# Float64 weights turned into float32 by three VectorE operations in place of four, with the top bits written by ScalarE as float16

## The chip, the cores and the metric

The kernel runs on one core of one Trainium2 chip. The time is that of one execution in device microseconds (us), the median over the runs. The engines are PE (TensorE matmul), PEld (its weight load), DVE (VectorE), ACT (ScalarE), POOL (GpSimd) and SP (SyncE, which issues every transfer here). Each engine takes its instructions in the order of its own list, and waits at one whose input or buffer is not ready.

## The reference

Three layers over 4 batches of 576 tokens: attention with rotated queries and keys (8 heads of 64), a gated channel layer (`k*k @ w_v` times a sigmoid gate), and a mixer (tokens, then channels) with a residual sum. The weights that matter for this change are drawn as `float32 * numpy float64 scalar`, so they arrive as float64:

```
'w_k': np.random.randn(d_model, d_ff).astype(np.float32) * (1.0 / np.sqrt(d_model))
k = np.maximum(xk @ w_k, 0.0);  v = k * k @ w_v;  r = 1 / (1 + np.exp(-(xr @ w_r)))
h = np.maximum(xt @ w_tok1, 0.0) @ w_tok2
h2 = np.maximum(u @ w_ch1, 0.0) @ w_ch2
```

All seven weight matrices have this form. [...]

## The kernel before, in words

Activations lie with the channels on the 128 partitions and 288 tokens (half a batch) along the free dimension. Every product of the two later layers is made from three matmuls on a high and a low half (`mm3`, L555: high by high, high by low, low by high), so each weight tile of 128 x 512 is also needed as a high half (`parts[:, 0]`, rounded) and a low half (`parts[:, 1]`, the rest).

The program is written stage by stage, but the order of the instructions on each engine is made by a list scheduler from readiness and priorities (`PRI`, `ahead`). A small edit can therefore move instructions that it does not touch.

Stages, in the order of time:

- Attention, 144 steps (`a_step`, L505), from 0 to about 465 us: scores on PE (L386), maximum on DVE (L392), exponential on ACT (L399), the two float16 halves of the probabilities on ACT (L75) and DVE (L418), transposes by DMA (L435), the product with the values on PE (L448). From about step 40 on, the matmuls of the gated layer's `k` and `v` (`kp`, `vp`) fill PE between the steps.
- The first weight conversion (`conv0`), beside the first steps of the attention: the 16 tiles of `w_k` and `w_v`.
- The second (`conv1`, 17 tiles: `w_r`, both token weights, the first six tiles of the channel weights), as the attention ends, with the rest of the gated layer. Then the token mixing of batch 0.
- The third (`conv2`, the 18 other channel tiles), beside the start of the last stage.
- The channel mixing (`c1p`, `co`), to the end.

A conversion (class `Conv`, L160) has four steps for each tile. Step 0 loads the raw words into the place that the finished halves will take (`words`, L182). Step 1 has ACT take the absolute value of the upper word, read as float32 (L190), into a buffer `v`. In step 2 DVE clamps it (L195), masks and shifts it (L197), puts sign and top exponent bit in (L199) and the top three bits of the lower word (L202). Step 3 has ACT round to the high half (L73 by way of `copy`) and DVE, or POOL in `conv0`, subtract to get the low half (L104). In `conv0` the buffer `v` is a PSUM bank (one, tag `acc`, shown as `cvp`), in the other two it is an SBUF tile (three, shown as `cv`); the raw words lie in SBUF throughout, so a word of every second 4 bytes is read.

Of the kernel before, what the change touches and what calls it, by code (L numbers as in the profile page):

```python
# [3 lines left out]

# [4 lines left out]
F32 = mybir.dt.float32  # L9
F32R = mybir.dt.float32r  # L10
F16 = mybir.dt.float16
I32 = mybir.dt.int32
I64 = mybir.dt.int64
ALU = mybir.AluOpType
AF = mybir.ActivationFunctionType
# [7 lines left out]
KD, KF, KC = DM // 128, DFF // 128, DCH // 128  # L23
PSCALE = 2.0 ** 14

F64_LEAST = struct.unpack("<f", struct.pack("<I", 0x38000000))[0]
F64_MOST = struct.unpack("<f", struct.pack("<I", 0x47EFFFFF))[0]

ND = 9

# [34 lines left out]
def body(tc, kin, qin, vw, tabs, ident, mu, w_k, w_v, w_r, w_t1, w_t2, w_c1, w_c2, out):  # L65
    nc = tc.nc
    PS = bass.MemoryType.PSUM
    act, dve, pool, pe, sp = nc.scalar, nc.vector, nc.gpsimd, nc.tensor, nc.sync

    def copy(e, o, i, scale=None):  # L70
        if e == "A":
            if scale is None:
                act.activation(out=o, in_=i, func=AF.Copy)  # L73
            else:
                act.activation(out=o, in_=i, func=AF.Copy, scale=scale)  # L75
        elif e == "P":
            pool.tensor_scalar(out=o, in0=i, scalar1=1.0 if scale is None else scale, scalar2=0.0,
                               op0=ALU.mult, op1=ALU.add)
        elif scale is None:
            dve.tensor_copy(o, i)  # L80
        else:
            dve.tensor_scalar(out=o, in0=i, scalar1=scale, scalar2=None, op0=ALU.mult)
# [20 lines left out]
    def tt(e, o, a, b, op):  # L103
        return (pool if e == "P" else dve).tensor_tensor(o, a, b, op=op)  # L104

    ctx = ExitStack()
    with ctx:
# [46 lines left out]
        def behind(o, name):  # L154

            if name in last:
                tc.add_manual_dep(o.ins, last[name].ins.name, mybir.DependencyInfo(
                    mybir.DependencyClass.NoSync, mybir.DependencyReason.DATA), reason="order")

        class Conv:  # L160
# [10 lines left out]
            def stage(self, j, i):  # L171
                if not 0 <= i < len(self.q):
                    return
                weights, k = self.q[i]
                src = weights.srcs[k]
                w = src.shape[1]
                wide = src.dtype == I64
                if j == 0:
                    raw = self.words[i] = weights.words(k)
                    if self.load:  # L180
                        behind(pool.memset(raw[:, 0:1], 0), self.load)
                    sp.dma_start(raw if wide else raw[:, :w], src.bitcast(I32))  # L182
                    return
                if j < 3:
                    hl = self.words[i].rearrange("p (a b) -> p a b", b=2)
                    lw, hw = hl[:, :, 0], hl[:, :, 1]
                if j == 1:
                    v = self.t[i] = (self.room or self.cv)()[:, :w]
                    if wide:
                        act.activation(out=v.bitcast(F32), in_=hw.bitcast(F32), func=AF.Abs)  # L190
                    else:
                        act.activation(out=v.bitcast(F32), in_=self.words[i][:, :w].bitcast(F32), func=AF.Copy)
                elif j == 2 and wide:
                    v = self.t[i]
                    yield lambda: dve.tensor_scalar(out=v.bitcast(F32), in0=v.bitcast(F32), scalar1=F64_LEAST,  # L195
                                                    scalar2=F64_MOST, op0=ALU.max, op1=ALU.min)
                    yield lambda: dve.tensor_scalar(out=v, in0=v, scalar1=0x07FFFFFF, scalar2=3, op0=ALU.bitwise_and,  # L197
                                                    op1=ALU.logical_shift_left)
                    yield lambda: dve.scalar_tensor_tensor(out=v, in0=hw, scalar=-0x40000000, in1=v,  # L199
                                                           op0=ALU.bitwise_and, op1=ALU.bitwise_or)  # L200
                    o = self.t[i] = self.cv()[:, :w] if self.room else v
                    yield lambda: dve.scalar_tensor_tensor(out=o, in0=lw, scalar=29, in1=v,  # L202
                                                           op0=ALU.logical_shift_right, op1=ALU.bitwise_or)
                elif j == 3:
                    dst, f = weights.take(k), self.t.pop(i).bitcast(F32)
                    copy("A", dst[:, 0], f)
                    tt(self.low, dst[:, 1], f, dst[:, 0].bitcast(F32), ALU.subtract)
# [737 lines left out]
        while not ch.done:  # L945
            b = n // (2 * KC)
# [73 lines left out]
```

## Time and profile before

| what | value |
|---|---|
| median of 3 runs | 993.18 us (988.93 to 996.47) |
| the profiled execution | 994.62 us, span 992.8 us |
| mean granted PE clock over the span | 0.953 |
| PE busy | 869.5 us (88%) |
| DVE busy | 587.5 us (59%) |
| ACT busy | 481.6 us (49%) |
| POOL busy | 421.4 us (42%) |

The span is what the trace covers; 1.8 us of the execution lie around it. A busy share is an average over stages that have different limits, so it is read stage by stage. [...]

### The profile page before, as it was taken

Reading aid. Unit: us, or ns where it says so; the run is one execution under the profiler, and the core shown is the slowest. Engines: PE = TensorE matmul, PEld = TensorE weight load, DVE = VectorE, ACT = ScalarE, POOL = GpSimd, SP = SyncE. Lnnn points to the kernel's source line nnn. Section 1 sums busy time; section 2 is a strip of 40 time slices with the busy share of each in tenths; the row PEclk is TensorE's granted clock in tenths of the full one; section 3 lists DMA queues with packets and bytes.
Section 4 is the critical chain, followed back from the end, with each engine's and each line's share of the span. In section 5 each row is a group of like instructions: output and inputs, shape, how many; then the busy total and the mean of one; then the engine's idle time right before and its main releaser. Section 6 shows DMA issues by size and latency. Waiting matters only on the chain.

```text
span 992.8 us, 17719 instructions
## 1 busy us (share of the span) xinstructions
PE 869.5 (88%) x6512; PEld 825.4 (83%) x6512; DVE 587.5 (59%) x1264; ACT 481.6 (49%) x1077; POOL 421.4 (42%) x448
## 2 busy tenths in 40 slices
PE   2645568888898988998889979999999999999997
PEld 2534456888788887997789979999999999999997
DVE  7998987777576687776995599532133211322121
ACT  3566576777576776785654555421142113211110
POOL 7456966777867587351645411410141013101010
PEclk9976577999999999999999989999999999999999
DMA  6999889999999998999910570110211001000000
GB/s 208 265 247 260 204 165 196 185 200 203 194 186 200 202 220 173 169 170 237 301 42 25 176 299 22 36 38 1 73 37 37 1 25 55 1 25 24 1 25 24
DMA packets 216182, 127.87 MB, mean 129 GB/s; under 512 B 176032, under 2 KB 194080, under 8 KB 215968
## 3 DMA queue, kind: packets, MB, share of 16 engines
q1 hardware_dynamic: 216096, 126.75, 54.2%
q8 instruction: 51, 0.84, 0.4%
q14 instruction: 35, 0.29, 0.1%
HBM read 60.90 MB, written 14.16 MB: 76 GB/s over the span
## 4 chain that ended last, share of the span: by engine, by line
PE 49%; DVE 7%; DMA 2%; issue 1%; ACT 1%; POOL 0%; SPq 0%; DVEq 0%; ACTq 0%
PE c1p L558 5%; PE c1p L559 5%; PE c1p L560 5%; PE co L558 5%; PE co L559 5%; PE co L560 5%; PE rp L558 2%; PE rp L559 2%; PE rp L560 2%; PE S L386 1%; DVE cv L199 1%; DVE cv L202 1%; DVE cv L195 1%; DVE parts L104 1%; PE vp L559 1%
## 5 line engine op out<-in xcount | busy, mean ns | idle before, releaser
L918 DVE SCALAR_TENSOR_TENSOR hs<-c1p,hs 128x288 fp32r<-128x288 f32 x96 | 43.6, 455 | 162.8 <-ACT hs L917 162.6
L399 ACT ACTIVATE S<-S,nm 128x576 f32<-128x576 f32 x144 | 102.5, 714 | 76.0 <-DVE nm L392 75.3
L917 ACT ACTIVATE hs<-c1p 128x288 fp32r<-128x288 f32 x96 | 38.9, 410 | 191.0 <-PE c1p L560 187.4
L418 DVE SCALAR_TENSOR_TENSOR p<-S,rc,p 128x576 f16<-128x576 f32 x144 | 114.5, 811 | 21.4 <-ACT p L75 20.4
L392 DVE TENSOR_REDUCE nm<-S 128x1 f32<-128x576 f32 x144 | 106.9, 750 | 29.5 <-PE S L386 29.0
L104 POOL TENSOR_TENSOR uhl<-y,uhl 128x288 fp32r<-128x288 f32 x32 | 25.5, 829 | 223.5 <-ACT uhl L73 223.5
L558 PE MATMUL c1p<-uhl,parts 128*128 128x288 f32 x384 | 115.2, 301 | 3.7 <-DVE y L104 3.7
L559 PE MATMUL c1p<-uhl,parts 128*128 128x288 f32 x384 | 114.8, 300 | 0.0
L560 PE MATMUL c1p<-uhl,parts 128*128 128x288 f32 x384 | 114.8, 299 | 0.0
L560 PE MATMUL co<-hs,parts 128*128 128x288 f32 x384 | 112.7, 296 | 0.0
L559 PE MATMUL co<-hs,parts 128*128 128x288 f32 x384 | 112.6, 296 | 0.0
L75 ACT ACTIVATE p<-S,rc 128x576 f16<-128x576 f32 x144 | 104.6, 751 | 14.7 <-issue 5.9
L558 PE MATMUL co<-hs,parts 128*128 128x288 f32 x384 | 108.1, 297 | 0.0
L386 PE MATMUL S<-kz,kq 128*128 128x288 f32 x576 | 96.7, 309 | 9.2 <-DVE p L418 5.2
L386 PE MATMUL S<-kq 64*128 64x288 f32 (+1 forms) x288 | 62.8, 389 | 43.6 <-DVE p L418 22.0
L386 PEld LDWEIGHTS S<-kz,kq 128*128 128x128 f32 x576 | 83.4, 195 | 16.4 <-issue 11.5
L386 PEld LDWEIGHTS S<-kq 64*128 64x128 f32 (+1 forms) x288 | 52.3, 257 | 52.4 <-issue 33.5
L558 PE MATMUL kp<-xs,parts 128*128 128x288 f32 x256 | 77.2, 309 | 13.2 <-ACT t L627 10.0
L448 PE MATMUL pv<-pt,vh 128*64 128x256 f16 (+1 forms) x576 | 51.0, 327 | 35.8 <-DMA pt<-p 31.8
L558 PE MATMUL vp<-k,parts 128*128 128x288 f32 x256 | 76.7, 302 | 4.4 <-ACT t L627 4.1
L559 PE MATMUL kp<-xs,parts 128*128 128x288 f32 x256 | 76.5, 300 | 3.4 <-POOL xs L104 3.2
L104 POOL TENSOR_TENSOR q<-t 128x288 f32<-128x288 f32 x64 | 48.4, 760 | 71.0 <-ACT t L627 44.6
(118 smaller groups left out, 2491.9 us busy)
## 6 DMA issues: line engine op xcount, KB each, us to landing
words<-in_w_c_dram SPq DMA_DIRECT2D x24, 512.0 KB, 6.8
rq<-in_qin_dram SPq DMA_DIRECT2D x30, 320.0 KB, 4.0
rk<-in_kin_dram SPq DMA_DIRECT2D x32, 288.0 KB, 4.1
kz<-kq SPq DMA_DIRECT2D x48, 144.0 KB, 2.9
vr<-in_vw_dram SPq DMA_DIRECT2D x16, 320.0 KB, 3.7
xd<-xT SPq DMA_DIRECT2D x16, 288.5 KB, 2.9
vd<-vt SPq DMA_DIRECT2D x32, 144.0 KB, 2.3
y<-vd SPq DMA_DIRECT2D x8, 576.0 KB, 5.3
```

The source lines that it names most:

```text
L75: act.activation(out=o, in_=i, func=AF.Copy, scale=scale)
L104: return (pool if e == "P" else dve).tensor_tensor(o, a, b, op=op)
L386: pe.matmul(p[:, h, 0:HS], lhsT=a[l, 128 * m:128 * m + 128], rhs=b[l, h * HS:(h + 1) * HS], start=(n == 0), stop=(n == 2))
L392: dve.tensor_reduce(out=nm, in_=S_t[j][:, :, 0:HS], op=ALU.max, axis=AX.XY, negate=True)
L399: act.activation(out=e, in_=e, func=AF.Exp, bias=sum_t[j], accum_out=s)
L418: dve.scalar_tensor_tensor(out=t[:, 1], in0=S_t.pop(j)[:, :, 0:HS], scalar=sum_t[j], in1=t[:, 0], op0=ALU.mult, op1=ALU.subtract)
L448: pe.matmul(p[l, 0:n], lhsT=v[:, a, l], rhs=ts[x][:, c, :], start=(i == 0), stop=(i == len(prods) - 1))
L558: pe.matmul(p, lhsT=wh, rhs=t[:, 0], start=first, stop=False)
L559: pe.matmul(p, lhsT=wh, rhs=t[:, 1], start=False, stop=False)
L560: pe.matmul(p, lhsT=wl, rhs=t[:, 0], start=False, stop=last)
L917: act.activation(out=h[:, 0], in_=p[:, 0:HS], func=AF.Relu)
L918: dve.scalar_tensor_tensor(out=h[:, 1], in0=p[:, 0:HS], scalar=0.0, in1=h[:, 0].bitcast(F32), op0=ALU.max, op1=ALU.subtract)
```

## The change: what it does

DVE masks and shifts the upper word straight from the loaded words (`hw`) into `v`; it was ACT's absolute value, clamped, that it masked before. ACT reads the same upper word as float32 and writes it back as float16, scaled by just under 1, over the top two bytes of that word, in place. The top five bits of that float16 are the sign and the top four exponent bits that the float32 needs. DVE then takes these five bits from the word (`TOP5`) and, as before, the top three bits of the lower word. The clamp is gone. The ACT instruction must come behind the first DVE one, since it overwrites what that reads, and the second DVE one behind ACT.

```
                 if j == 1:
-                    v = self.t[i] = (self.room or self.cv)()[:, :w]
+                    v = self.t[i] = (self.room if self.room and wide else self.cv)()[:, :w]
                     if wide:
-                        act.activation(out=v.bitcast(F32), in_=hw.bitcast(F32), func=AF.Abs)
+                        top = self.words[i].bitcast(F16).rearrange("p (a b) -> p a b", b=4)[:, :, 3]
+                        dve.tensor_scalar(out=v, in0=hw, scalar1=0x00FFFFFF, scalar2=3, op0=ALU.bitwise_and,
+                                          op1=ALU.logical_shift_left)
+                        act.activation(out=top, in_=hw.bitcast(F32), func=AF.Copy, scale=JUST_UNDER)
...
                 elif j == 2 and wide:
                     v = self.t[i]
-                    yield lambda: dve.tensor_scalar(out=v.bitcast(F32), in0=v.bitcast(F32), scalar1=F64_LEAST,
-                                                    scalar2=F64_MOST, op0=ALU.max, op1=ALU.min)
-                    yield lambda: dve.tensor_scalar(out=v, in0=v, scalar1=0x07FFFFFF, scalar2=3, op0=ALU.bitwise_and,
-                                                    op1=ALU.logical_shift_left)
-                    yield lambda: dve.scalar_tensor_tensor(out=v, in0=hw, scalar=-0x40000000, in1=v,
-                                                           op0=ALU.bitwise_and, op1=ALU.bitwise_or)
+                    yield lambda: dve.scalar_tensor_tensor(out=v, in0=hw, scalar=TOP5, in1=v, op0=ALU.bitwise_and,
+                                                           op1=ALU.bitwise_or)
```

In the changed kernel these are L190 (DVE mask and shift), L192 (ACT), L197 and L200 (DVE); lines behind them are two lower than before, lines ahead of them one lower.

The scheduler places the instructions anew. On DVE, the sixth tile of `w_k` in `conv0`, beside attention steps. Before:

```order
L195 TENSOR_SCALAR cvp<-cvp 128x512
L392 TENSOR_REDUCE nm<-S 128x1 x2
L406 TENSOR_SCALAR den<-S 128x1
L197 TENSOR_SCALAR cvp<-cvp 128x512
L407 RECIPROCAL rc<-den 128x1
L406 TENSOR_SCALAR den<-S 128x1
L199 SCALAR_TENSOR_TENSOR cvp<-words,cvp 128x512
L407 RECIPROCAL rc<-den 128x1
L406 TENSOR_SCALAR den<-S 128x1
L202 SCALAR_TENSOR_TENSOR cv<-words,cvp 128x512
```

The changed kernel:

```order
L190 TENSOR_SCALAR cvp<-words 128x512
L103 TENSOR_TENSOR kq<-rq,kq 128x640
L197 SCALAR_TENSOR_TENSOR cvp<-words,cvp 128x512
L200 SCALAR_TENSOR_TENSOR cv<-words,cvp 128x512
L390 TENSOR_REDUCE nm<-S 128x1
```

Between the tile's first and second DVE instruction, where ACT must do its part, stands one other instruction; over the 51 tiles it is one to six. The last tile of `conv0` is finished on DVE behind 28 of the maxima `nm`, where it was 34 before.

On DVE, the first tiles of `conv1` (`w_r`), with the last attention steps between them. Before:

```order
L195 TENSOR_SCALAR cv<-cv 128x512
L82 TENSOR_SCALAR xT<-pv,sc 128x256
L197 TENSOR_SCALAR cv<-cv 128x512
L418 SCALAR_TENSOR_TENSOR p_6512<-S,rc,p_6512 128x576
L392 TENSOR_REDUCE nm<-S 128x1
L199 SCALAR_TENSOR_TENSOR cv<-words,cv 128x512
L195 TENSOR_SCALAR cv<-cv 128x512 x2
L202 SCALAR_TENSOR_TENSOR cv<-words,cv 128x512
```

The changed kernel:

```order
L190 TENSOR_SCALAR cv<-words 128x512
L81 TENSOR_SCALAR xT<-pv,sc 128x256
L416 SCALAR_TENSOR_TENSOR p_6496<-S,rc,p_6496 128x576
L390 TENSOR_REDUCE nm<-S 128x1
L190 TENSOR_SCALAR cv<-words 128x512
L197 SCALAR_TENSOR_TENSOR cv<-words,cv 128x512
L190 TENSOR_SCALAR cv<-words 128x512
L404 TENSOR_SCALAR den<-S 128x1
L200 SCALAR_TENSOR_TENSOR cv<-words,cv 128x512
```

The two operations on `cv` alone have become one that reads `words`; the rest of the piece stands in the same order.

## Rows read from the trace of the kernel before

**Rows 1.** Page, busy time of each engine (us, share of the span, instructions).
```profile
PE 869.5 (88%) x6512; PEld 825.4 (83%) x6512; DVE 587.5 (59%) x1264; ACT 481.6 (49%) x1077; POOL 421.4 (42%) x448
```
**Rows 2.** Stretches: busy us of PE, PEld, DVE, ACT, POOL; PE clock; DMA; GB/s.
```profile
25.00:140.00 115.00, 67.26 (x384) 56.13 (x382) 103.08 (x220) 68.83 (x139) 74.60 (x65) 0.73 0.99 234
140.00:460.00 320.00, 285.53 (x2295) 262.99 (x2295) 233.99 (x540) 226.69 (x503) 206.83 (x218) 0.97 0.95 192
460.00:520.00 60.00, 48.28 (x360) 43.44 (x359) 55.41 (x104) 37.85 (x85) 31.79 (x32) 1.00 0.64 190
562.00:594.00 32.00, 26.15 (x185) 25.21 (x183) 28.68 (x58) 19.93 (x43) 9.17 (x10) 0.94 0.79 296
600.00:993.00 393.00, 387.69 (x2941) 385.93 (x2939) 118.66 (x255) 98.36 (x244) 61.15 (x72) 1.00 0.08 25
```
**Rows 3.** Groups of instructions, conv0: busy us, mean ns; idle time before them, releaser.
```profile
L195 DVE TENSOR_SCALAR cvp<-cvp 128x512 f32<-128x512 f32 x16 | 11.0, 687 | 2.2 <-ACT cvp L190 2.2
L197 DVE TENSOR_SCALAR cvp<-cvp 128x512 int32<-128x512 int32 x16 | 11.1, 692 | 0.2
L202 DVE SCALAR_TENSOR_TENSOR cv<-words,cvp 128x512 int32<-128x512 int32 x16 | 10.8, 675 | 0.0
L190 ACT ACTIVATE cvp<-words 128x512 f32<-128x512 f32 x16 | 10.1, 630 | 6.2 <-DVE cv L202 4.9 <-DMA words<-in_w_k_dram 1.3
```
**Rows 4.** Groups by shape, the 512-wide tiles of conv1 and conv2.
```profile
L195 DVE TENSOR_SCALAR cv<-cv 128x512 f32<-128x512 f32 x28 | 13.7, 491 | 5.4 <-ACT cv L190 5.4
L197 DVE TENSOR_SCALAR cv<-cv 128x512 int32<-128x512 int32 x28 | 13.9, 504 | 0.0
L199 DVE SCALAR_TENSOR_TENSOR cv<-words,cv 128x512 int32<-128x512 int32 x28 | 21.3, 768 | 0.0
L190 ACT ACTIVATE cv<-words 128x512 f32<-128x512 f32 x28 | 18.9, 679 | 14.7 <-DVE parts L104 10.0 <-DMA words<-in_w_r_dram 3.8 <-DMA words<-in_w_c_dram 0.5
```
**Rows 5.** Stretches, the instructions of L195 alone: length, DVE busy us.
```profile
25.00:140.00 115.00, 10.99 (x16) 0.73 0.99 234
460.00:520.00 60.00, 8.51 (x17) 1.00 0.64 190
562.00:594.00 32.00, 4.65 (x9) 0.94 0.79 296
```
**Rows 6.** Line L195 from 460 us on: duration min/median/max ns, first and last start.
```profile
L195 DVE TENSOR_SCALAR cv<-cv x27: 278/415/1012, 466.9 to 596.8; 128x512 f32<-128x512 f32 x20, 128x256 f32<-128x256 f32 x5, 128x576 f32<-128x576 f32 x2
```
**Rows 7.** Timeline of DVE in conv1: start us, us, operation.
```profile
507.46 0.68 DVE L202 SCALAR_TENSOR_TENSOR cv<-words,cv 128x512 int32<-128x512 int32 x1
508.06 0.41 DVE L195 TENSOR_SCALAR cv<-cv 128x512 f32<-128x512 f32 x1
508.39 0.75 DVE L197 TENSOR_SCALAR cv<-cv 128x512 int32<-128x512 int32 x2
```
**Rows 8.** Waits from 25 to 140 us: total us, times, longest.
```profile
ACT S L399 <- DVE nm L392: 26.7, 19, 4.3
PE S L386 <- DVE p L418: 17.0, 10, 6.4
```
**Rows 9.** Waits from 460 to 600 us.
```profile
ACT cv L190 <- DVE parts L104: 13.0, 11, 2.8
ACT parts L73 <- DVE cv L202: 11.7, 14, 1.5
PE kp L558 <- ACT t L627: 8.0, 7, 2.1
DVE cv L195 <- ACT cv L190: 4.5, 2, 3.3
```
**Rows 10.** Chain that ended last, as batch 0's mixing is released: start us, us, what.
```profile
592.54 0.93 DVE cv L195
593.47 0.38 DVE y L104
593.98 0.58 PE c1p L558
```

More of the change, by code (lines that the diff above doesn't have):

```diff
@@ L1 @@
-import struct
 from contextlib import ExitStack
@@ L24 @@
 PSCALE = 2.0 ** 14
-F64_LEAST = struct.unpack("<f", struct.pack("<I", 0x38000000))[0]
-F64_MOST = struct.unpack("<f", struct.pack("<I", 0x47EFFFFF))[0]
+TOP5 = -0x08000000
+JUST_UNDER = 1.0 - 2.0 ** -12
 ND = 9
```

## The prediction

> **What bounds the kernel now.** I read the busy shares first, then the same by stretches, since no engine is full over the whole span [rows 1]. The stretches show four regimes [rows 2]. From 600 us to the end PE is busy 387.7 of 393 us, so nothing that DVE saves there is worth anything. From 140 to 460 us PE is busy 285.5 of 320 us and DVE only 234: PE is the nearest to full. But in the three stretches where weights are converted DVE is the fullest engine: 103.1 of 115 us from 25 to 140, 55.4 of 60 from 460 to 520, 28.7 of 32 from 562 to 594. The reader is to see that the conversion, a side job, sits just where DVE decides.
>
> The waits say the same. In the first of these stretches ACT's exponentials wait 26.7 us for DVE's maxima and PE's scores wait 17.0 us for DVE to free their bank [rows 8]: both are DVE instructions queued behind conversions. Around 460 to 600 us ACT's conversion steps wait 13.0 and 11.7 us for DVE, ACT's own queue is held by that, and PE waits 8.0 us for an eviction in that queue (`kp` by `t`) [rows 9]. And the chain that ended last runs, just before the channel mixing may start, through a clamp L195 of 0.93 us, then the last sum `y`, then PE's first `c1p` matmul [rows 10]: the removed kind of instruction stands on the path itself.
>
> **The change part by part.** For each of the 51 tiles DVE loses the clamp L195 and keeps three instructions; ACT keeps its number; transfers, POOL's work and PE's work are the same in number. I cost DVE by start-to-start distance, since consecutive instructions overlap: the 0.68 us L202 is followed after 0.60, the 0.41 us L195 after 0.33 [rows 7], so each removed one frees 0.08 us less than its duration.
>
> *conv0, 16 tiles.* L195 took 0.687 us each, 10.99 in all [rows 3, 5]; 16 x (0.687 - 0.08) = 9.8 us. The mask and shift now reads SBUF and writes PSUM. No row has exactly that; between PSUM and PSUM it took 692 ns, and L202, which reads both, 675 [rows 3]. I take 692, so no change. DVE is busy 103.1/115 = 0.90 of the stretch, and I let that share of the saving reach the end of it: 8.8 us. If DMA or POOL set the pace instead it is 0, if DVE does so alone 9.8. It then has to survive the 320 us behind it: the work there is the same and merely starts earlier.
>
> *conv1, 17 tiles.* L195 took 8.51 us in the stretch [rows 5], less 17 x 0.08 is 7.2, by the busy share 0.92 it is 6.6. Here PE is next late: it is idle 60 - 48.3 = 11.7 us [rows 2], and of that 8.0 is the wait for an eviction that DVE holds up [rows 9]. I take 8.0/11.7 = 0.68 of it: 4.5 us. Bounds: 0, if those evictions are late anyway, and 11.7, if all of PE's gaps close.
>
> *conv2, the 9 tiles whose clamp falls before the mixing starts.* 4.65 us [rows 5], less 9 x 0.08 is 3.9, by 28.7/32 it is 3.5 us. DVE is on the chain here [rows 10] and PE is idle 5.8 us [rows 2], so 3.5 fits in; bounds 0 and 5.8. The other 9 clamps lie where PE is full, or nearly: nothing.
>
> *The price of the new mask and shift in SBUF.* It reads every second word where L197 read a dense tile. The nearest rows are that same operation on a dense tile, median 0.41 us on L195's form [rows 6] and mean 0.50 with its long ones [rows 4], and the strided L202, 0.68 where nothing disturbs it [rows 7]. I take the dense price, as L202 has a second tensor. At 0.68, and in proportion for the five narrow tiles and the two wide ones [rows 6], conv1 loses 10 x 0.68 + 5 x 0.34 + 2 x 0.77 - 8.51 = 1.5 us of its 8.51, conv2 9 x 0.68 - 4.65 = 1.5, and with the shares above the gain shrinks by about 2.3 us. [...] No row of the kernel before shows a strided single source.
>
> *ACT.* It wrote to PSUM in 630 ns in conv0, to SBUF in 679 later [rows 3, 4]; now always SBUF. 16 x 0.05 is 0.8 us on an engine that is 60% busy there [rows 2]: nothing on the path. It writes 2 bytes in every 8, which no row shows; bounded by the row below, 0.63, and, with no reason to exclude it, by twice 0.68. Hidden as long as DVE has other work meanwhile.
>
> *The added waits.* DVE's first instruction waits for the load; ACT's waits for DVE; DVE's second waits for ACT. Behind ACT's waiting instruction stand exponentials and evictions, behind DVE's the maxima. On the other side, DVE no longer waits for ACT at L195, 2.2 us in conv0 and 4.5 later [rows 3, 9]. The order shows one to six DVE instructions between the two that flank ACT, mostly two or more, so I take these two to balance: 0. Bound: 42 tiles on the path (16 + 17 + 9) by a full 0.65 us, 27.
>
> Sum: 8.8 + 4.5 + 3.5 = 16.8 us off the profiled execution's 994.6, which is **978**. The median of the runs shown is 993.2, 1.4 lower, well inside the range below.
>
> **The rivals.**
>
> *The first stage isn't DVE's.* DMA's share from 25 to 140 us is 0.99 [rows 2], and the tiles are packed into 28 attention steps where it was 34, so loads come denser. Then the 8.8 falls away and 4.5 + 3.5 stay: 994.6 - 8.0 = 987. Against: the waits of ACT and PE there name DVE [rows 8].
>
> *All of PE's gaps close.* 9.8 + 11.7 + 5.8 = 27.3: 967. For: ACT's waits for DVE, 24.7 us in all [rows 9], are longer than what I credit. Against: PE waits for loads and transposes too.
>
> *The order gives it back.* The scheduler shuffles the stretch from 140 to 460 us, where PE is busy 0.89 of the time [rows 2]. At 0.85 it takes 285.5/0.85 = 336 us, 16 more: 994. For: many rows move. Against: the work and its dependences there are the old ones.
>
> *Slower: DVE stands at the second instruction until ACT has written.* The place is L197 of the changed kernel. If nothing covers ACT's 0.65 us, 42 tiles cost 27.3 us, against 16.8 saved: 994.6 + 10.5 = 1005. It decides once DVE stands more than 16.8/42 = 0.40 us per tile. A slow 2-byte write on ACT would lead here too. For: one instruction can be all that stands between, and ACT itself may be late, holding exponentials meanwhile. Against: most gaps in the order hold more than an ACT duration, as a maximum or a probability half.
>
> *The change doesn't do what it says.* The DVE list has 51 instructions fewer, one per tile, so this is out.
>
> **How the numbers follow.** Chances: the forecast 0.45, first stage not DVE's 0.18, all gaps close 0.15, order gives it back 0.12, slower 0.10. The predicted time is that of the likeliest, 978. The range goes from 966, just below the second rival, to 993, and leaves out the slower case (0.10) and about half of the one at 994, with a rest of 0.02. What a measurement here can tell from no change is about 1%, 9.9 us, so faster means below 983.3 and slower above 1003.1. Faster: 0.44 of the forecast, 0.15, and 0.02 of the rival at 987, together 0.61. Slower: 0.10. The rest is 0.29.
>
> **What would show it right or wrong.** [...] Idle time of DVE before L197, ended by ACT, of more than some 15 us would show the slower case at work. The prediction is wrong if the first stage ends no earlier, or if it does and the stretch behind it grows.

## The result, and the profile after

The changed kernel takes 1005.53 us (median, 1002.94 to 1005.93) where the kernel before took 991.1 us (988.93 to 996.47) beside it: a ratio of **1.0126, interval 1.01 to 1.0153**. By the ratio it is slower by some 12.5 us; the forecast was 978. The profiled execution took 1005.93 us, with a span of 1004.2 us. Of all runs below only one, of `g_conv0` (1001.24 us), fell into a slower state of the chip, and it is left out.

The page of the changed kernel, answering [rows 1]:

```profile
PE 885.1 (88%) x6512; PEld 830.0 (83%) x6512; DVE 571.3 (57%) x1213; ACT 507.6 (51%) x1077; POOL 415.4 (41%) x448
```

DVE has its 51 instructions fewer and 16 us less to do. But ACT has 26 us more, with the same number of instructions, and PE 16 us more, with the same number of matmuls. The second is the stranger one: nothing in the change touches a matmul.

The same stretches as [rows 2] (busy us of PE, PEld, DVE, ACT, POOL; PE clock; DMA; GB/s), for the changed kernel:

```profile
25.00:140.00 115.00, 67.78 (x357) 53.63 (x356) 98.17 (x202) 78.84 (x138) 76.09 (x71) 0.68 0.95 228
140.00:460.00 320.00, 286.09 (x2245) 259.38 (x2245) 229.06 (x532) 221.71 (x493) 203.91 (x212) 0.96 0.94 188
460.00:520.00 60.00, 52.31 (x357) 45.43 (x356) 49.22 (x85) 41.02 (x75) 27.38 (x29) 0.89 0.76 213
```

In the first stretch DVE is less full (98.2 us for 103.1) and ACT fuller (78.8 for 68.8). In the second PE is as busy as before, 286 us, but gets through 2245 matmuls in place of 2295. In the third PE spends 52.3 us on 357 matmuls, where it spent 48.3 on 360, and its mean granted clock there, as a share of full speed, is 0.89 for 1.00.

The groups of the conversion (busy us, mean ns; idle time before them and its releaser), answering [rows 3, 4]. A float64 weight is two 32-bit words; `words` holds both, and the upper one has the sign, the exponent and the top of the fraction.

```profile
L192 ACT ACTIVATE words<-words 128x512 f16<-128x512 f32 x44 | 59.2, 1380 | 9.9 <-DVE cvp L190 5.0 <-DVE cv L190 4.8
...
L197 DVE SCALAR_TENSOR_TENSOR cvp<-words,cvp 128x512 int32<-128x512 int32 x16 | 11.1, 692 | 5.3 <-ACT words L192 5.2
L190 DVE TENSOR_SCALAR cvp<-words 128x512 int32<-128x512 int32 x16 | 10.9, 682 | 0.0
```

The ACT instruction takes 1,380 ns, twice the 630 and 679 of before. DVE stands 5.2 us in `conv0` for it, and 4.0 us later at the 512-wide tiles. The mask and shift has the prices that I took: 682 ns into PSUM, and in SBUF, by line L190:

```profile
L190 DVE TENSOR_SCALAR cv<-words x35: 279/417/1031, 476.1 to 627.4; 128x512 int32<-128x512 int32 x28, 128x256 int32<-128x256 int32 x5, 128x576 int32<-128x576 int32 x2
```

Its median of 417 ns, with every second word read, is that of the clamp on a dense tile, 415 [rows 6]; at the 512-wide tiles its mean is 505 ns, where the dense mask and shift took 504 [rows 4].

Waits of the changed kernel (total us, times, longest) from 25 to 140 us, answering [rows 8]:

```profile
PE S L384 <- DVE p L416: 26.4, 8, 9.2
...
ACT S L397 <- DVE nm L390: 14.8, 12, 2.6
```

and from 460 to 600 us, answering [rows 9]:

```profile
PE kp L556 <- ACT t L625: 6.2, 5, 2.9
```

ACT waits 12 us less for DVE's maxima, as a lighter DVE should bring. But PE's scores wait 9 us longer for the bank that `p` frees. `p` on DVE needs ACT's half (L74) first, so the slow ACT step could be behind that; but `e1_wide` below, which has the same order and a fast ACT step, still waits 23.7 us there. Most of the 9 us goes with the order. The `kp` matmuls wait for ACT's evictions nearly as long as before (6.2 us for 8.0).

A few points of time say where the loss arose. The first `kp` matmul starts at 120.1 us where it started at 139.4: the conversion of the first stage did end earlier. The attention beside it gained nothing by that: its 31st to 55th maximum (of 144) start between 4.8 us earlier and 5.3 us later than before, most within 3 us (the 41st at 156.1 us for 158.5), the 101st at 340.3 for 342.1. Then the 131st starts at 437.5 us, where it was 426.1, and the last at 477.9 for 468.7: **by the maxima some 13 us are lost between 340 and 437 us, where no weight is converted.** About half of that is work left over from before. Between the 71st and the 101st maximum PE took up 154 matmuls `vp` in place of 192 (first the kernel before, then the changed one; busy us of PE, PEld and ACT with `vp`, then PE clock, DMA, GB/s):

```profile
251.50:342.10 90.60, 29.18 (x192) 27.13 (x192) 3.35 (x8) 0.98 0.95 192
252.00:340.30 88.30, 22.41 (x154) 20.85 (x155) 2.54 (x6) 0.98 0.99 193
```

Up to the 131st maximum it did 136 where it had done 96, and 28 more of the values' matmuls: at 0.14 and 0.07 us each some 7 us. So the loss is spread over 250 to 437 us. And the first `c1p` matmul starts at 606.4 us for 594.0; from there to the end nothing differs.

PE's list in that stretch shows what is new. First the kernel before (start us, us, operation, count; in brackets idle time):

```profile
345.60 1.41 PE L448 MATMUL pv<-pt,vh 128*64 128x320 f16 x18 [0.89 <-DMA pt<-p]
346.82 0.87 PE L448 MATMUL pv<-pt,vl 128*64 128x320 f16 x10
347.62 1.06 PE L386 MATMUL S<-kz,kq 128*128 128x288 f32 x6
348.52 0.29 PE L558 MATMUL kp<-xs,parts 128*128 128x288 f32 x1
```

and the changed kernel at a like place:

```profile
351.88 0.40 PE L384 MATMUL S<-kz,kq 128*128 128x288 f32 x1
352.21 0.32 PE L446 MATMUL pv<-pt,vh 128*64 128x320 f16 x1
352.46 0.40 PE L384 MATMUL S<-kz,kq 128*128 128x288 f32 x1
352.79 0.32 PE L446 MATMUL pv<-pt,vh 128*64 128x320 f16 x1
353.05 0.40 PE L384 MATMUL S<-kz,kq 128*128 128x288 f32 x1
```

The scheduler has interleaved one score matmul with one values' matmul. Start to start, such a pair takes 353.05 - 352.46 = 0.59 us. Apart, by the rows of before, a values' matmul takes (346.82 - 345.60)/18 = 0.068 us and a score matmul (348.52 - 347.62)/6 = 0.150, together 0.218. So a pair costs 0.37 us more, or about 0.18 us for each change from one kind to the other. Some of that is not the change: by their single records in the trace of before, two of the values' matmuls start 3 to 31 ns apart and the next two 0.14 us after the first two, so that each costs 0.07 us; one that stands alone between scores has no partner and loses, by my estimate from these gaps, about 0.07. What is left is 0.15 for each change. I counted the changes between values' matmuls and others in the traces, from 0 to 500 us: 98 before, 142 in the changed kernel. If all 44 were of this kind, they would be 44 x 0.15 = 7 to 44 x 0.18 = 8 us.

### The profile page after: what moved, and what is told of

Its sections match the earlier page's. It is cut to its first block, busy times and chain, and to the rows that moved or that the text cites. A ratio compares the mean times of both kernels' runs of the same rounds, so it can differ in the third digit from the quotient of the medians.

```text
span 1004.2 us, 17689 instructions
## 1 busy us (share of the span) xinstructions
PE 885.1 (88%) x6512; PEld 830.0 (83%) x6512; DVE 571.3 (57%) x1213; ACT 507.6 (51%) x1077; POOL 415.4 (41%) x448
## 4 chain that ended last, share of the span: by engine, by line
PE 53%; DVE 5%; ACT 3%; issue 3%; DMA 3%; POOL 2%; SPq 0%; DVEq 0%; ACTq 0%; POOLq 0%
PE c1p L556 5%; PE co L556 5%; PE co L557 5%; PE co L558 5%; PE c1p L557 5%; PE c1p L558 5%; PE S L384 3%; PE pv L446 2%; PE rp L556 2%; PE rp L557 2%; PE rp L558 2%; PE kp L556 1%; PE vp L556 1%; PE vp L557 1%; PE vp L558 1%
## 5 line engine op out<-in xcount | busy, mean ns | idle before, releaser
L384 PE MATMUL S<-kz,kq 128*128 128x288 f32 x576 | 99.6, 310 | 17.3 <-DVE p L416 9.8
L74 ACT ACTIVATE p<-S,rc 128x576 f16<-128x576 f32 x144 | 103.9, 750 | 17.6 <-issue 9.0
L384 PE MATMUL S<-kq 64*128 64x288 f32 (+1 forms) x288 | 64.9, 396 | 46.8 <-DVE p L416 30.9
L556 PE MATMUL kp<-xs,parts 128*128 128x288 f32 x256 | 81.6, 325 | 16.7 <-ACT t L625 12.6
L103 POOL TENSOR_TENSOR q<-t 128x288 f32<-128x288 f32 x64 | 45.2, 709 | 88.3 <-ACT t L625 62.9
L557 PE MATMUL kp<-xs,parts 128*128 128x288 f32 x256 | 79.6, 312 | 1.5 <-POOL xs L103 1.4
L558 PE MATMUL kp<-xs,parts 128*128 128x288 f32 x256 | 78.7, 309 | 0.0
```

What stands on the lines that cost most here:

```text
L384: pe.matmul(p[:, h, 0:HS], lhsT=a[l, 128 * m:128 * m + 128], rhs=b[l, h * HS:(h + 1) * HS], start=(n == 0), stop=(n == 2))
L556: pe.matmul(p, lhsT=wh, rhs=t[:, 0], start=first, stop=False)
L557: pe.matmul(p, lhsT=wh, rhs=t[:, 1], start=False, stop=False)
L558: pe.matmul(p, lhsT=wl, rhs=t[:, 0], start=False, stop=last)
```

## The experiments

My theories after the result were two. The **write**: ACT's instruction is slow because it writes 2 bytes in every 8. The **order**: the scheduler mixes two kinds of matmul on PE, and each change costs. The rival to both was that the added waits between DVE and ACT take the time.

In the table, changes are those on PE counted in the trace, and PE's busy and idle time runs from 0 to its first token-mixing matmul, with the same work in all. Each ratio is to runs of the kernel before that were made beside it. The last three columns come from one execution each, and executions of one kernel differ by several us (29 of the kernel before lie between 986.36 and 1000.81), so a few us between two rows of these columns show little. The profiled execution was the slowest of the four of `p_before` and the fastest of `p_after` and of `v_pair0_g`.

| kernel | median us (runs) | ratio to before, interval | changes | PE busy, idle us | first `c1p` |
|---|---|---|---|---|---|
| before | 991.1 to 994.95 | 1 | 98 | 439.6, 112.2 | 594.0 |
| changed | 1005.53 (4) | 1.0126, 1.0100 to 1.0153 | 142 | 456.5, 107.6 | 606.4 |
| e1_wide | 999.08 (12) | 1.0043, 1.0015 to 1.0071 | 142 | 454.2, 105.1 | 599.2 |
| e2_conv0 | 1002.5 (10) | 1.0083, 1.0052 to 1.0114 | 144 | 459.0, 100.3 | 601.1 |
| e3_conv12 | 996.02 (10) | 1.0021, 0.9988 to 1.0053 | 96 | 445.8, 111.3 | 598.6 |
| g_before | 997.1 (12) | 1.0042, 1.0017 to 1.0066 | 96 | 444.9, 109.3 | 595.7 |
| g_after | 993.45 (12) | 1.0006, 0.9978 to 1.0034 | 98 | 443.9, 108.6 | 594.1 |
| g_wide | 989.74 (12) | 0.9966, 0.9941 to 0.9992 | 98 | 444.8, 104.0 | 590.0 |
| p_before | 1009.32 (4) | 1.0171, 1.0131 to 1.0211 | 142 | 460.5, 110.1 | 612.9 |
| p_after | 1008.63 (4) | 1.0155, 1.0112 to 1.0199 | 78 | 440.1, 121.6 | 605.0 |
| v_pair | 999.7 (6) | 1.0068, 1.0046 to 1.0091 | 120 | 445.8, 108.3 | 598.0 |
| v_pair_g | 991.34 (10) | 0.9983, 0.9961 to 1.0006 | 96 | 446.3, 101.3 | 591.8 |
| g_conv0 | 992.26 (11) | 0.9993, 0.9971 to 1.0015 | 98 | 442.7, 105.5 | 590.0 |
| g_conv12 | 995.74 (12) | 1.0037, 1.0018 to 1.0055 | 96 | 444.9, 111.1 | 597.4 |
| v_pair0_g | 987.23 (11) | 0.9957, 0.9936 to 0.9979 | 98 | 440.0, 103.2 | 584.6 |

### The price of the write by itself

`m1_prices` is the kernel before with copies of 512 elements behind its end, one change from line to line:

```
+        for _ in range(4):
+            act.activation(out=hd, in_=st, func=AF.Copy)   # and o8, h4, h8, in place; DVE, POOL
```

> The kernel before, with a row of copies added behind its end that use nothing but prices: ACT and DVE copies of 512 elements per partition, read at every second word or dense, written as float32 or float16, dense, at every second 2-byte place, at every fourth, and in place. The changed kernel's ACT write took 1380 ns where the old ACT step took 630 to 680. Theory 'two-byte places': float16 at every fourth place takes about 1.4 us in a tile of its own too, float16 written dense and float32 at every second word about 0.68. Rival 'in place': only the write over the words that are being read is slow, the same write into another tile takes about 0.68. Rival 'conversion': every float16 output is slow, the dense one too.

Measured (groups by shape: busy us, mean ns; idle before):

```profile
L981 ACT ACTIVATE oa<-y 128x512 f16<-128x512 f32 x4 | 5.3, 1334 | 0.1
...
L979 ACT ACTIVATE oa<-y 128x512 f16<-128x512 f32 x4 | 3.1, 774 | 0.1
...
L987 DVE CAST oa<-y 128x512 f16<-128x512 f32 x4 | 2.9, 736 | 27.7 <-ACT oa L985 27.6
L995 ACT ACTIVATE y<-y 128x512 f16<-128x512 f32 x2 | 2.7, 1336 | 0.1
...
L977 ACT ACTIVATE oa<-y 128x512 f16<-128x512 f32 x4 | 2.6, 654 | 0.1
L973 ACT ACTIVATE oa<-y 128x512 f32<-128x512 f32 x4 | 2.6, 652 | 0.1
...
L989 DVE CAST oa<-y 128x512 f16<-128x512 f32 x4 | 1.8, 456 | 0.1
```

All of ACT's lines here read every second word. Float16 written densely (L977) takes 654 ns, 4 bytes written every 8 (L973) 652. Float16 written every 4 bytes (L979) takes 774, every 8 bytes 1,334 (L981) with a tile of its own and 1,336 in place (L995). So it is neither the conversion, nor the stride of whole words, nor that it writes where it reads: it is 2-byte values that lie apart, and 8 bytes far more than 4. On DVE it is 456 ns at 4 bytes (L989) and 736 at 8 (L987), on POOL 1,317 at 8.

### The write and the stages, in the changed kernel

`e1_wide` writes the whole word, in the same order of instructions (DVE then takes other bits as the top five, so it computes other weights):

```
-                        act.activation(out=top, in_=hw.bitcast(F32), func=AF.Copy, scale=JUST_UNDER)
+                        act.activation(out=hw.bitcast(F32), in_=hw.bitcast(F32), func=AF.Copy, scale=JUST_UNDER)
```

> The changed kernel with one thing changed: ACT writes the whole upper word as float32 in place and not its top two bytes as float16, so the top bits are wrong and the output with them; every engine's order of instructions is the same as in the changed kernel. Theory 'price': the loss comes from ACT's 1380 ns; then this write takes about 0.68 us and the time falls to what was forecast, 975 to 983 against 991 of before (ratio 0.985 to 0.992). Rival 'order': the new order of instructions and the hand-overs from DVE to ACT and back cost it, however long ACT takes; then the time stays at 1000 to 1006 (ratio 1.01 to 1.015). In between, both have a part.

Its ACT group is back at the old price:

```profile
L192 ACT ACTIVATE words<-words 128x512 f32<-128x512 f32 x44 | 29.6, 680 | 15.3 <-DVE cv L190 9.9 <-DVE cvp L190 5.3
```

The ratio is 1.0043 where the changed kernel has 1.0126: the write costs 0.8%, some 8 us (good to about 4), in this order. In the changed kernel's chain that ended last it can be seen on the path while `conv2` runs (start us, us, what):

```profile
579.12 0.59 ACT words L192
...
580.73 1.28 ACT words L192
...
589.68 0.71 ACT words L192
...
599.22 0.22 ACT words L192
...
600.77 1.28 ACT words L192
```

4.1 us of 44, where the chain of the kernel before has 1.4 us of ACT's old step (L190) in the 44 us up to its first `c1p`. But e1_wide is still no faster than before, so the write is not the whole of it.

`e2_conv0` and `e3_conv12` convert the new way in `conv0` alone, or in the two later stages alone:

```
+                    if wide and not (self.room):          # e3: not (not self.room)
+                        act.activation(out=v.bitcast(F32), in_=hw.bitcast(F32), func=AF.Abs)
+                    elif wide:
...
+                    new = self.room                       # e3: not self.room
+                    if not new:
+                        (the old clamp, mask and shift)
```

> The new conversion in conv0 alone (w_k and w_v, beside the attention), the old one of four DVE operations in conv1 and conv2. In the changed kernel the last maximum of the attention came 9 us later than before, the first matmul of the channel mixing 12 us later. If the loss arises in conv0, this one has most of it: about 1000 (ratio 1.009). Rival: the 9 us come about where conv1 begins, or from the order of the stretch between; then this is 985 to 992, no slower than before, since DVE saves 11 us in conv0.

> The new conversion in conv1 and conv2 alone, the old one in conv0. If the loss arises in conv0, this has the rest of it: about 994 (ratio 1.003). If it arises where the attention ends and conv1 runs, about 1003 (ratio 1.012).

Measured 1.0083 and 1.0021. With `conv0` alone PE's idle time falls by 12 us, the most of all runs in which nothing else is changed, and yet the kernel is slower: PE's busy time rises by 19, with 144 changes. With the later stages alone the count is 96 and little moves. The loss comes by way of `conv0`, mostly through the order behind it.

One piece lies inside `conv0`, and the write has no part in it. The product `kq` on DVE, 17 times (duration min/median/max ns), first before, then in the changed kernel:

```profile
L104 DVE TENSOR_TENSOR kq<-rq,kq x17: 807/825/1759, 14.3 to 416.7; 128x640 fp32r<-128x640 f32 x15, 128x256 fp32r<-128x256 f32 x1, 128x384 fp32r<-128x384 f32 x1
L103 DVE TENSOR_TENSOR kq<-rq,kq x17: 798/1266/5171, 13.1 to 423.0; 128x640 fp32r<-128x640 f32 x15, 128x256 fp32r<-128x256 f32 x1, 128x384 fp32r<-128x384 f32 x1
```

and PE at that place in the changed kernel (start us, us, operation, count; in brackets idle time):

```profile
115.92 1.78 PE L384 MATMUL S<-kq 64*128 64x288 f32 x6 [5.00 <-DVE den L404]
```

One of the 17, from 109.8 to 115.0 us, takes 5.2 us, while POOL has four of its own products one behind the other; PE stands idle for 5.0 us until DVE is past it. e1_wide and e2_conv0 have the same (5.6 and 4.8 us), the runs with the rule below none above 2.1, except `v_pair0_g` (3.6). That POOL is the cause is a guess from this timing: no run takes it away.

### The price of a change on PE

`m2_switch` appends runs of matmuls in turn to the kernel before, 24 of each kind, 288 columns of input each:

```
+        for _ in range(24):
+            f32()       # 128 wide, float32
+            f16n()      # 64 wide, float16; then f32/f16w, f32/f32n, f16w/f16n
```

> The kernel before, with PE matmuls of 288 columns added behind its end that use nothing but time: 24 of the scores' kind (float32, 128 weight columns), 24 of the values' kind (float16, 64 weight columns), then 24 pairs that alternate: float32 wide with float16 narrow, float32 wide with float16 wide, float32 wide with float32 narrow, float16 wide with float16 narrow. In the changed kernel's trace a score matmul that stands between two of the values' takes 0.33 us to the next start and the other 0.25, where in runs of their own kind they take 0.13 and 0.07. Theory 'change of type': only the alternations of float32 with float16 cost, about 0.38 us per pair beyond the two alone. Rival 'change of width': the two alternations of wide with narrow cost it too, of whatever type. Rival 'waits': here, with nothing to wait for, no alternation costs anything.

Its timeline, in the order of the runs: each alone, then in turn.

```profile
985.12 3.46 PE L968 MATMUL m<-uhl,parts 128*128 128x288 f32 x24
988.51 2.76 PE L972 MATMUL m<-oh 128*64 128x288 f16 x21
...
991.57 0.40 PE L968 MATMUL m<-uhl,parts 128*128 128x288 f32 x1
991.90 0.31 PE L972 MATMUL m<-oh 128*64 128x288 f16 x1
992.14 0.40 PE L968 MATMUL m<-uhl,parts 128*128 128x288 f32 x1
...
1008.71 0.39 PE L968 MATMUL m<-uhl,parts 128*128 128x288 f32 x1
1008.95 0.30 PE L974 MATMUL m<-oh 128*128 128x288 f16 x1
1008.99 0.39 PE L968 MATMUL m<-uhl,parts 128*128 128x288 f32 x1
...
1014.31 0.30 PE L970 MATMUL m<-uhl,parts 128*64 128x288 f32 x1
1014.45 0.29 PE L968 MATMUL m<-uhl,parts 128*128 128x288 f32 x1
1014.58 0.30 PE L970 MATMUL m<-uhl,parts 128*64 128x288 f32 x1
...
1022.37 0.30 PE L974 MATMUL m<-oh 128*128 128x288 f16 x1
1022.60 0.31 PE L972 MATMUL m<-oh 128*64 128x288 f16 x1
1022.84 0.30 PE L974 MATMUL m<-oh 128*128 128x288 f16 x1
```

Alone, the wide float32 one takes (988.51 - 985.12)/24 = 0.141 us and the narrow float16 one (991.57 - 988.51)/24 = 0.128. A pair of these takes 992.14 - 991.57 = 0.57, which is 0.30 too much, or 0.15 for a change. Wide float32 beside wide float16 takes 0.28 a pair and wide beside narrow float32 0.27: no cost. Wide beside narrow float16 takes 0.47, where 0.14 (0.28 - 0.14) and 0.13 would be 0.27: 0.10 for a change. So the cost is neither one of type nor one of width alone. In these rows it comes where a float16 matmul of 64 columns stands beside one of 128, and the values' matmuls are of that kind (`128*64`). What PE does in the added time no run shows.

### The same conversions in a like order

`g_before`, `g_after` and `g_wide` are the kernel before, the changed one and e1_wide with one more rule for the scheduler: no score matmul inside a block of values' matmuls, and none of these inside a block of scores.

```
+                    o = pe.matmul(p[:, h, 0:HS], ...)     # scores; the values' likewise
+                    behind(o, "pv")
+            last["S"] = o
```

> The kernel before with one more rule for the scheduler: a score block and a values block on PE may not be mixed (each starts behind the other's last matmul, in the order in which the program names them). Changes from the values' matmuls to others and back: 96, as before (98). If such changes are what matters, the time is that of before, 985 to 998 (ratio 0.995 to 1.005).

> The changed kernel with the same rule; 98 changes on PE instead of 142. Theory 'changes': 44 fewer at 0.19 us are 8.4 us, so 1005.5 - 8.4 = 997 (ratio about 1.004 to before). Rival 'the rest of the order': it stays at 1.01 or above.

> As g_after, but ACT writes the whole upper word as float32 (0.68 us; the top bits and the output are wrong). Theory: with both causes taken away, the slow write and the changes on PE, what is left is the forecast's gain of DVE, as far as it exists: 999.1 - 8.4 = 990.7, ratio about 0.996; the full forecast would be 0.984. Rival: it stays at 1.004, then the changes on PE cost nothing.

Measured 1.0042, 1.0006 and 0.9966. The rule costs the old conversion 0.4% and gives the new one 1.2%, 12 us. At 96 to 98 changes throughout, the new conversion is now 0.36% better than the old one, and with the 4-byte write 0.76%, 7.5 us. So DVE's relief is real, the write takes about half of it, and the order took more than all of it. The orders are alike in the count alone: no run puts the old conversion into the changed kernel's very order.

Is it the count of changes? `p_before` and `p_after` change the count by one figure of the scheduler's table instead:

```
-PRI = dict(den=50, hi=400, pv=20, ...                 # old conversion, p_before
+PRI = dict(S=30, den=50, hi=400, pv=20, ...
...
-PRI = dict(den=50, hi=400, pv=20, ...                 # new conversion, p_after
+PRI = dict(den=50, hi=400, pv=300, ...
```

> The old conversion, with one figure of the scheduler's table changed: the score blocks come 30 places earlier. The order that results has 142 changes on TensorE between values' matmuls and others, as many as the new conversion's order (the kernel before has 98). Theory (the changes themselves cost, about 0.19 us each): 44 x 0.19 = 8.4 us, ratio to before 1.007 to 1.010, TensorE's busy time up to the output projection 8 us or more above 439.8. Rival (changes are only a sign of late score blocks; what costs is the new conversion): 0.998 to 1.003.

> The new conversion as it is, with one figure of the scheduler's table changed (the values' matmuls go 300 places earlier instead of 20), which gives 78 changes in place of 141. Theory: 63 x 0.19 = 12 us less than the new conversion has, so a ratio to before of about 1.000 (0.997 to 1.003), as the rule of the grouped blocks gave by another way (1.0006). Rival (the rule helped by something else that it does to the order): 1.008 or more.

`p_before` bears the theory out and goes beyond it: the old conversion with 142 changes is at 1.0171, and PE's busy time grows by 21 us, part of it at a lower granted clock (0.89 up to the token mixing, 0.93 before). No new conversion is needed to lose that much. `p_after` misses: with 78 changes it is at 1.0155.

From the changed kernel's 456.5 PE's busy time fell by 16 us with the count, as it should, to 440.1. But PE stands 14 us longer. The largest part is the values' matmuls, which now wait longer for the transposed probabilities (total us, times, longest, up to the token mixing):

```profile
PE pv L446 <- DMA pt<-p: 29.6, 19, 5.3
```

In the changed kernel this wait is 19.9 us.

So PE's busy time goes with the count of changes (454 to 461 us at 142 to 144, 440 to 446 at 78 to 120), but the kernel's time does not by itself: an order with few changes can stand elsewhere. The theory that the changes alone decide is too simple; that the order decides is what stands.

### What is left of each term, and a version that is faster

ACT can write each float16 twice, side by side, so that every 32-bit word of a tile of its own is written whole, and DVE takes the top bits from there. It then no longer writes over what DVE's first instruction reads, so ACT need not wait for DVE either; these runs change both at once. `v_pair` does so everywhere, `v_pair_g` with the rule of the blocks:

```
-                        top = self.words[i].bitcast(F16).rearrange("p (a b) -> p a b", b=4)[:, :, 3]
+                        top = v.bitcast(F16).rearrange("p (a b) -> p a b", b=2)
...
-                        act.activation(out=top, in_=hw.bitcast(F32), func=AF.Copy, scale=JUST_UNDER)
+                        act.activation(out=top, in_=hw.bitcast(F32).unsqueeze(2).broadcast_to([128, w, 2]), ...)
```

> A correct version that keeps the three operations, but lets ScalarE write its float16 values twice next to each other, so that every 32-bit word of a tile of its own is written whole; VectorE then takes the top bits from that tile. 1,024 elements written densely: about 1.1 us by 630 ns for 512 (1.38 in the new conversion). Its order has about 120 changes. Theory: 22 changes fewer x 0.19 = 4 us and a quarter of the 8 us that the spaced write cost, so a ratio to before of about 1.006 (1.002 to 1.009). If only the write counts: 1.010 or more.

> v_pair with the rule that score blocks and values' blocks are not mixed on TensorE (about 96 changes). Theory: between the new conversion with that rule (1.0006) and the one with a 4-byte write (0.9966): 0.997 to 1.001. If it is under 0.996 it beats all correct versions so far.

Both came in as expected, 1.0068 and 0.9983. The last three ask what the terms are worth in a like order: `g_conv0` and `g_conv12` are e2_conv0 and e3_conv12 with the rule, `v_pair0_g` is `g_conv0` with the paired write.

> The new conversion in conv0 alone, the old one elsewhere, and score blocks and values' blocks not mixed on TensorE: about 98 changes, as in the kernel before. Forecast: 1.0042 (the same rule with the old conversion everywhere) less conv0's term. If that term has its size of 8.8 us, the ratio to before is 0.995; if the spaced write of ScalarE takes a part of it, as the step times of the run with the rule showed (5 to 7 us left), 0.997 to 0.999; if conv0 gives nothing, 1.004.

> The new conversion in conv1 and conv2 alone, with the same rule (about 96 changes). If conv1's and conv2's terms have their size (4.5 and 3.5 us), 1.0042 - 0.008 = 0.996; if ScalarE's spaced write, which takes 28 x 0.7 us longer there, eats them, 1.002 to 1.006.

> As g_conv0, but ScalarE writes each float16 value twice, side by side, into a tile of its own (1.06 us a tile for 1.38). Forecast: g_conv0 less some 2 us (16 x 0.3 us, half of it on the path): 0.995 to 0.998. If it is the best so far, conv0 is where the change is worth something.

Measured 0.9993, 1.0037 and 0.9957. Against `g_before` (1.0042) `conv0` gives 0.49%, 4.9 us, with the spaced write, and 0.85%, 8.4 us, with the paired one; the two later stages give 0.05%, 0.5 us. These differences of two ratios are good to about 0.3 points, 3 us. Nor do the later stages gain by the paired write: with it in all stages the ratio is 0.9983, with it in `conv0` alone 0.9957. `v_pair0_g` has the lowest ratio of all and beats the kernel before by 0.2 to 0.6%. Its page, and its ACT group in `conv0`:

```profile
PE 867.5 (88%) x6512; PEld 818.9 (83%) x6512; DVE 576.5 (59%) x1248; ACT 489.1 (50%) x1077; POOL 428.4 (44%) x448
```

```profile
L195 ACT ACTIVATE cv<-words 128x1024 f16<-128x1024 f32 x16 | 16.9, 1059 | 9.7 <-DMA words<-in_w_k_dram 6.3 <-DMA words<-in_w_v_dram 3.2 <-POOL parts L106 0.2
```

1,024 values written densely take 1,059 ns, less than the 1,380 of 512 spaced ones in the changed kernel. ACT's step now waits for the loads and no longer for DVE (5.0 us in `conv0` of the changed kernel), and PE is back at 867.5 us.

## Why the prediction was wrong

Its forecast fell, in three steps of different weight.

**The step that failed most is the one behind `conv0`:** "It then has to survive the 320 us behind it: the work there is the same and merely starts earlier." The matmuls are the same, their order is not, and on PE the order has a price: from the 101st maximum to the last the attention fell from 1.9 us ahead to 9.2 behind. The step ahead of it, that 8.8 us reach the end of the stage, failed in this order too: the 35th to 55th maximum stood about where they were. In a like order both hold: against `g_before`, `g_conv0` has its 41st maximum 2.2 us earlier and its last 5.5, `v_pair0_g` 7.0 and 11.0. The rival "the order gives it back" had the right place and nearly the right size (16 us forecast; 12 by the rule), the size by luck: it had PE standing more, 0.85 busy for 0.89, and PE was as busy as before and did 50 matmuls fewer. It had the chance of 0.12 for a poor reason: I held against it that the work and its dependences are the old ones, and never looked at how the two kinds of matmul lie in PE's list. The changes could be counted in the built order of both kernels before anything ran; their price was not to be had from the trace of before without looking for it.

**ACT's write** was bounded rightly, "by twice 0.68", and came out at that bound, 1.38. What failed is "hidden as long as DVE has other work meanwhile". I priced it only as a wait of DVE, and DVE's wait at L197 is indeed small: 5.2 us in `conv0` and 4.7 later, under the 15 I had named, and before it had stood 2.2 and 4.5 at L195 [rows 3, 9]. So the slower rival's mechanism, DVE standing, was not at work, and that its time of 1005 was hit is luck, though its remark on a slow 2-byte write was right. ACT has 26 us more to do, and taking the slow write away gives back 8 us in the order of the changed kernel and 4 with the rule. By which wait it reaches the end is shown only in part: on the chain of `conv2`. That exponentials and evictions behind the write in ACT's queue pass on the rest is argued.

**The terms.** `conv0`'s 8.8 (16 x 0.607 is 9.7 and not 9.8, so 8.7) was right in size in a like order: 4.9 with the spaced write, 8.4 with the paired one, which also frees ACT from waiting for DVE. "First stage not DVE's" is thereby out. The 8.0 of `conv1` and `conv2` came to 0.5. In `conv1` PE's idle time did close, from 11.7 to 7.7 us of 60, close to the 4.5 I had credited, but its busy time grew by the same 4.0 for 357 matmuls in place of 360, at the lower clock (and the window holds other work, as the attention ended 9 us later). The stretch was not 4.5 us shorter in any run: from the last maximum to the first token-mixing matmul it took 83.1 us before, 85 to 92 in the other runs with the old conversion there, and 84 to 93 with the new one. In `conv2` the write stands on the chain; e1_wide, without it, has 39.9 us from the first token-mixing matmul to the first `c1p`, where before has 42.2 and the changed kernel 42.3: 2.3 of the forecast 3.5. With the rule even that is not seen: `g_wide` has 41.2 and `g_before` 41.5.

Right were: DVE's 51 instructions, the mask and shift at 0.68 and 0.42 us, and the balance of DVE's own waits. DVE's busy time fell by 16 us: the durations of the conversion's instructions fell by 27 in all, but the 17 products `kq` took 8.5 us more (26.4 for 18.0), and the rest is small changes and overlap. The first `kp` matmul came 19 us earlier, where 8.8 us were to reach the end of the stage.

**The sum, by ratios:** the rule takes away 1.20%, the write (with the rule) 0.40%; what is left stands at 0.9966. 11.9 + 4.0 - 3.4 = 12.5 us, the loss that was measured. Each term is the difference of two neighbours, so the sum closes by itself and is no test. Measured from `g_before`, the old conversion with the rule, the relief is 7.5 us and the order's part 16: -7.5 + 4.0 + 16 = 12.5. That the order takes 12 to 16 us is shown; what in it does so is not settled. 44 changes at 0.15 to 0.18 us are 7 to 8. The long `kq` held PE for 5.0 us once; how much of that reaches the end no run tells, and `v_pair0_g` has one of 3.6 and the lowest time. PE's busy time rose by 17 in all, part of it at a lower granted clock (0.90 up to the token mixing, 0.93 before): e3_conv12, with 96 changes and 0.90, has 445.8 us, 6 more than before and 11 less than the changed kernel. The runs with the rule have 0.90 to 0.92 as well, so the clock is not what sets the two apart. And `p_after` shows that an order with few changes can be as slow.

## What to carry to other kernels

Under a list scheduler, an edit to one engine is judged only when the order on the bound engine is alike: count there, in the built order, what stands next to what before and after, and run the old version in an order like the new one's and the new in one like the old one's. The count warns, but does not give the time: 78 changes were here as slow as 142. And where a cheap operation moves to another engine with an odd output pattern, price that one instruction by itself first: here 2-byte values 8 bytes apart took ACT 1,334 ns, where it wrote them densely in 654. The same bits written as whole words, in a like order and in the first stage alone, gave a kernel 0.4% faster than before.

## What the runs showed of the hardware that was not expected

- Writing 2-byte values 8 bytes apart took ACT twice as long as writing them densely, and DVE 1.6 times as long as 4 bytes apart. ACT, 512 elements: 654 ns dense, 774 every 4 bytes, 1,334 every 8; whole 4-byte words every 8 bytes, 652. DVE 456 every 4 and 736 every 8. POOL took 1,317 at 8 bytes, with nothing to compare.
- In `m2_switch` a float16 matmul of 64 columns next to one of 128 cost PE 0.10 us for each change (0.47 us a pair), next to a float32 one of 128 columns 0.15 (0.57 a pair); float32 ones of 64 columns next to 128 cost nothing (0.27 a pair).
- One and the same product on DVE, `kq` of 128 x 640, took from 0.80 to 5.17 us in the changed kernel; the longest ran while POOL had four products one behind the other.
- The granted clock fell in the changed kernel as the attention ended, and not in the kernel before, though PE had gaps in both. Stretches of 5 us, the changed kernel:

```profile
480.00:485.00 5.00, 3.11 (x16) 2.76 (x17) 5.00 (x9) 4.72 (x9) 2.37 (x3) 0.76 1.12 220
485.00:490.00 5.00, 4.44 (x19) 4.09 (x18) 4.77 (x9) 3.36 (x6) 2.69 (x3) 0.50 0.65 155
```

and the kernel before:

```profile
465.00:470.00 5.00, 2.58 (x18) 2.12 (x16) 3.06 (x6) 3.05 (x6) 1.58 (x2) 1.00 1.20 285
470.00:475.00 5.00, 2.51 (x16) 2.28 (x17) 5.00 (x12) 3.75 (x10) 2.23 (x3) 1.00 1.00 204
```

In the changed kernel the mean clock is 0.76 of full speed in a stretch in which PE was busy 3.1 of 5 us, and 0.50 in the next; in the kernel before it stays at 1.00 through two stretches with 2.6 and 2.5. Why the one fell and the other did not, no run here tells.
